# Filter in 64-row tiles and a folded first sequence: a Hyena convolution followed by routed experts on one Trainium2 core

## The chip, the cores and the metric

The kernel runs on one core of a Trainium2 chip. The core has a matrix engine (TensorE, PE in the rows; its weight loads are PEld), a vector engine (VectorE, DVE), a scalar engine (ScalarE, ACT), a general engine (GpSimd, POOL) and a queue engine that issues most DMAs (SyncE, SP). Each engine works through its own instructions in order; semaphores tie them together. The metric is the device time of one execution in microseconds.

## The reference

Two layers follow each other. The first is a long convolution over four sequences of 11456 tokens with 128 channels; the second sends every token to one of eight experts.

```python
h_mlp = np.maximum(pos_emb @ w1, 0.0) @ w2          # [S, 64] -> [S, 128]
h_filt = h_mlp * np.exp(-0.01 * pos)[:, None]
u = x * v
y = irfft(rfft(u, 2 * S) * rfft(h_filt, 2 * S))[:, :S, :]
x = (x * y).reshape(B * S, D)
logits = x @ w_gate + modality_bias[modality_id]
e_idx = argmax(logits); gate_w = softmax(logits)[e_idx]
out[e_idx == e] = gate_w * (np.maximum(x[e_idx == e] @ w1[e], 0.0) @ w2[e])
```

All inputs are float32, and the float32 matmuls of the convolution run on TensorE as two passes each: a weight load and a stream of moving columns, twice.

## The kernel before

**Transform.** The convolution is done by a two-step transform of length 90 x 64. A sequence lies as 2 blocks (`blk`) of 90 x 64 tokens, of which 45 pairs of places are held: partition `n` (0 to 63, 45 in use) has place `n`, and partition `64 + n` the mirrored place. The first step is a product with `fwd` (two halves, `c`, of 90 columns): the even part of the cosine table is the same for a place and its mirror, the odd part has the opposite sign (`shape_constants`). So one contraction over 128 partitions forms, in effect, sum and difference of the two halves and transforms them. The second step (`middle_stages`) works on groups of four of the 90 frequencies.

**Stages and their order.** The program is a list of steps, `seq`; a step calls small functions that issue instructions, and the order of these calls is each engine's order. The stages of the start are:

1. The filter's outer part (`filter_stages`, lines 515 to 551), 16 values of `q`. `load(q)` fetches 256 KB of embeddings on SP. `hidden(q)` multiplies with `wf[:, 1]`, in which w1 stands twice on the diagonal, 128 rows (line 528: four matmuls of 128 weight columns and 128 moving columns), and one DVE instruction applies ReLU and the window and leaves PSUM (line 532). `transform(q)` multiplies by `fwd` (line 542: four matmuls of 180 moving columns), and ACT copies the result to `A` (line 547). By `FOUT` a step issues load(t), hidden(t - 2) and transform(t - 3), in that order.
2. The filter's middle (`filter_middle`, lines 574 to 615), 23 groups: turn (line 581), spectrum (591, with the table B that `load_b` fetched into `A`, line 571), second (606, 64-row tiles, with w2 from `wf[:, 0]`); ACT and DVE copy (583, 594, 609 to 611), and POOL's queue writes each group's spectrum to DRAM (`hs`, line 612).
3. The forward transform of sequence 0 (`forward_stages(0)`, lines 480 to 514), 16 values of `q`. `load(q)` issues four DMAs on SP (lines 486 and 487, two each for u and v). `product(q)` is one DVE instruction, u times v (line 492). `transform(q)` does two halves, each 16 matmuls of 128 rows, 64 weight columns and 90 moving columns into a pair of PSUM banks (line 507), and ACT copies the half to `A` (line 510). There are two pairs of banks. Loads and products lie `F2` = 24 steps earlier, beside the filter's middle; there are 12 tiles for u and six halves of three output tiles (`xo`) for v.

`load_b(k)` stands in step k of `seq`, from 0 to 22. The memsets of `wg`, of three `xo` tiles and of twelve tiles (lines 441 to 445) are POOL's first work.

Then follow the middle stage of sequence 0 (`middle_stages(0)`), and for each further sequence its forward transform, middle stage, inverse transform and routing, interleaved. Routing writes rows to DRAM, and POOL scatters them to the experts' regions (`send_rows`).

**Experts.** `experts` works through tiles of 512 rows, eight chunks each (`hidden`, `result`). `rows_in(i + 2)` fetches rows on SP; `result` writes a tile's output to DRAM by four DMAs (line 1271) and reads it back turned (`y`, line 1273); ACT scales it two tiles later (line 1290), and POOL scatters it. Where a tile's rows lie stands in tables that DVE makes by some twenty short instructions each (`tile_table`). They are generators: at each chunk the loop takes one step of one of them (`next`), and `rows_in` runs them out when a tile needs its table. The last one, `rest()`, writes eight pads behind the experts' rows (lines 1052 to 1062) and then makes the last two tables.

Of the kernel before, what the change touches and what calls it, by code (L numbers as in the profile page):

```python
# [15 lines left out]
I32 = mybir.dt.int32  # L16
# [45 lines left out]
FMID = "turn:0 spectrum:1 second:3"  # L62
FIRST = "forward load product"
EA = 3
# [9 lines left out]
def apart(a, axis):  # L74

    out = np.zeros_like(a)
    n = np.arange(HALF)
    to, of = [slice(None)] * a.ndim, [slice(None)] * a.ndim
    to[axis], of[axis] = 4 * (n // 3) + n % 3, n
    out[tuple(to)] = a[tuple(of)]  # L80
    return out


# [16 lines left out]
def shape_constants():  # L100
# [28 lines left out]

    win = apart(win.reshape(2, 64, 2, N2), 1).transpose(2, 1, 3, 0)  # L130

# [59 lines left out]
def hyena_moe_kernel(ctx: ExitStack, tc: tile.TileContext, a: dict, out: bass.AP,  # L191
# [189 lines left out]
    with ExitStack() as cv:  # L381
# [25 lines left out]
        wf = keepp.tile([D, 2, D], F32, name="wf")  # L407
        dve.memset(wf, 0.0)
        wg = late_wg
# [15 lines left out]
        def constants():  # L425
            sp.dma_start(inv, a["c_inv"].rearrange("p (c n) -> p c n", c=2))
            sp.dma_start(small, a["c_small"])
            t = counts["tri"] = new_a("tri")[:, 0:2 * D]
            sp.dma_start(t, a["c_tri"])
            sp.dma_start(wg[:, 0:E], a["moe_w_gate"])  # L430
            sp.dma_start(bias, a["moe_modality_bias"].rearrange("m e -> (m e)")
                         .partition_broadcast(D).rearrange("p (m e) -> p m e", m=2))

        def split_constants():
            dve.tensor_copy(base, sm("reg"))
            dve.tensor_copy(score[:, E], sm("bad"))
            dve.memset(powers[:, E], 1e-9)
            dve.tensor_copy(both, counts.pop("tri"))
            free("tri")
# [35 lines left out]
        def forward_stages(b):  # L475
# [37 lines left out]

            return load, product, transform

        def filter_stages():
# [7 lines left out]
            def hidden(q):  # L524
                t = kept.pop((q, "emb"))
                m1 = bank("m1")
                for i in range(4):
                    pe.matmul(m1[:, D * i:D * i + D], t[:, D * i:D * i + D], wf[:, 1],
                              start=True, stop=True)
                free(("emb", q))  # L530
                r = new_a(("r", q))[:, 0:512].rearrange("p (m f) -> p m f", m=8)
                dve.scalar_tensor_tensor(
                    r, m1.rearrange("p (m f) -> p m f", m=8), 0.0,
                    win[:, q].unsqueeze(2).broadcast_to([D, 8, D // 2]),
                    op0=ALU.max, op1=ALU.mult)
                kept[q, 1] = r.rearrange("p (n b) f -> p n (b f)", b=2)

            def transform(q):
                r = kept.pop((q, 1))
                p = pair("s1")  # L540
                for j in range(4):
                    pe.matmul(p[:, j // 2, 2 * N1 * (j % 2):2 * N1 * (j % 2 + 1)],
                              r[:, j], fwd.rearrange("p c k -> p (c k)"), start=True, stop=True)
                free(("r", q))
                for h in range(2):
                    n0 = 4 * q + 2 * h
                    act.copy(A[:, :, 0].rearrange("p k (c n) -> p k c n", c=2)[:, :, :, n0:n0 + 2],
                             p[:, h, 0:4 * N1].rearrange("p (n c k) -> p k c n", n=2, c=2))

# [350 lines left out]
        def outer_steps(b):  # L900
# [13 lines left out]
            if b < nb:  # L914
                load, product, transform = forward_stages(b)
                todo |= {"load": load, "product": product, "forward": transform}
            if b == nb:
                todo.pop("places")
# [11 lines left out]
            if b == 0:  # L930
                ahead = lambda q: 2 * q if q < NA else q + F2 - NA
                when = {"load": ahead, "product": lambda q: ahead(q) + 2, "forward": lambda q: q + F2 - 1}
                return steps(NQ, [(when[n], todo[n]) for n in FIRST.split()])
            table = [w.split(":") for w in (LAST if b == nb else OUTER).split()]
# [113 lines left out]
    def rest():  # L1048


        assert not waiting and len(scatters) == nb * NR // D, (len(waiting), len(scatters))
        sp.dma_start(pad, a["c_pad"].rearrange("p (j r) -> p j r", j=TH // D))
        sp.dma_start(xs[E * R:E * R + TH, :].rearrange("(p j) r -> p j r", j=TH // D), pad)
        end = new("step", [1, E], I32)
        dve.tensor_copy(end, base[0:1])
        yield
        for e in range(E):
            v = nc.values_load(
                end[0:1, e:e + 1], engines=[ENG.SP], min_val=0, max_val=E * R - TH,
                skip_runtime_bounds_check_because="a region holds every token and a tile more")  # L1060
            after_all(sp.dma_start(xs[ds(v, TH), :].rearrange("(p j) r -> p j r", j=TH // D), pad),
                      scatters)
            yield
        dve.tensor_sub(nall, base[0:1], reg)
# [11 lines left out]
        tabs[nb] = new("tabh", [1, 3, NH], I32)  # L1076
        yield from tile_table(new, tabs[nb], took, start, left, NH, TH)

    outs, fetched = [], []
# [13 lines left out]
    def experts(lo, hi):  # L1093
# [212 lines left out]
        for at in range(len(work) + 6):  # L1306
# [45 lines left out]
def device_inputs(inputs):  # L1352
    arrays = {name: np.ascontiguousarray(inputs[name]) for name in _INS}
    tile4 = lambda a: a.reshape(D, 2, NQ, 4, -1).transpose(2, 0, 1, 3, 4).reshape(NQ, D, -1)
    held = np.r_[0:D:2, 1:D:4]
    chan8 = lambda a: (apart(a.reshape(2, 64, 2, N2, NQ, 8), 1).transpose(4, 2, 1, 0, 5, 3)
                       .reshape(NQ, D, -1)[:, held])
    for name, of, order in (("x", "x", tile4), ("u", "x", chan8), ("v", "v", chan8)):
        arrays[name] = np.ascontiguousarray(
            np.stack([order(spread(np.asarray(a))) for a in inputs[of]]))  # L1360

    pos = apart(spread(np.asarray(inputs["pos_emb"])).reshape(2, 64, 2, NQ, 4, -1), 1)
    arrays["pos_emb"] = np.ascontiguousarray(
        pos.transpose(3, 0, 5, 4, 2, 1).reshape(NQ, D, -1))
    ids = np.asarray(inputs["moe_modality_id"]).astype(np.int64, copy=False).reshape(B, S)
# [22 lines left out]
```

## Time and profile before

| what | value |
|---|---|
| median of 3 runs | 2089.98 us (2086.85 to 2091.12) |
| the profiled execution | 2090.39 us |
| its span, first to last instruction | 2088.5 us |
| PE, PEld, DVE, ACT, POOL busy | 97%, 79%, 80%, 60%, 62% |
| granted TensorE clock, mean | 0.994 |

The profile is that of one execution. An engine is busy while one of its compute instructions runs; matmuls are pipelined, so one's duration is longer than its distance to the next, and a stretch counts as busy when any runs. In the groups a line gives the source line, the engine, the operation, output and input, the shape and the count; behind the bar the busy time and the mean of one in ns, then the idle time before them and what ended it.

### The profile page before, as it was taken

The page shows a single profiled execution, that of the slowest core. Times are in us where ns is not written, and L with a number is a line of the kernel's source. Part 1 is how long each engine was busy: PE and PEld are TensorE (multiplying, and loading weights), DVE is VectorE, ACT ScalarE, POOL GpSimd, SP SyncE. Part 2 cuts the span into 40 slices and gives each one's busy share as a digit, 9 for nine tenths or more (in the row PEclk, how much of TensorE's full clock was granted, in tenths as well). Part 3 has the DMA queues.
Part 4 walks back from the last instruction along what each step waited for, and adds up shares of the span by engine and source line. Part 5 has one row for each costly group of instructions (what it writes and reads, how often), then busy time and mean ns, then how long its engine had stood idle before and what let it go on. Part 6 is the DMA issues. An engine that isn't in the chain of part 4 may idle for free. (4 is left out here: it accounts for less than half of the span.)

```text
span 2088.5 us, 50278 instructions
## 1 busy us (share of the span) xinstructions
PE 2020.7 (97%) x17794; PEld 1651.2 (79%) x17794; DVE 1670.4 (80%) x2690; ACT 1262.1 (60%) x2454; POOL 1286.7 (62%) x1426
## 2 busy tenths in 40 slices
PE   8999999999999999999999999999999899999997
PEld 8887877777778777777578888888888778888897
DVE  2528777896779867896987898888888798888885
ACT  3642376225752376325666777777777677777775
POOL 2219700697868777786758777777776344444554
PEclk9999999999999999999999999999999999999999
DMA  9846766668877788765896567666665555555310
GB/s 292 308 163 230 246 207 193 224 235 278 277 233 248 251 263 279 246 238 166 242 307 204 118 134 149 136 142 143 136 147 109 106 101 93 98 97 102 81 42 28
DMA packets 502937, 380.78 MB, mean 182 GB/s; under 512 B 374745, under 2 KB 408365, under 8 KB 502681
## 3 DMA queue, kind: packets, MB, share of 16 engines
q1 hardware_dynamic: 470265, 294.16, 52.1%
q0 software_dynamic: 32256, 83.33, 12.0%
q8 instruction: 142, 2.33, 0.5%
q14 instruction: 114, 0.93, 0.1%
q10 hardware_dynamic: 160, 0.03, 0.0%
HBM read 273.80 MB, written 103.96 MB: 181 GB/s over the span
## 5 line engine op out<-in xcount | busy, mean ns | idle before, releaser
L1242 DVE SCALAR_TENSOR_TENSOR hl<-ph,hh 128x512 fp32r<-128x512 f32 x724 | 489.7, 684 | 120.3 <-ACT hh L1241 109.1
L1294 POOL DMA_INDIRECT out<-ot,idx x362 | 389.6, 1076 | 295.7 <-issue 230.1
L1241 ACT ACTIVATE hh<-ph 128x512 fp32r<-128x512 f32 x724 | 422.9, 595 | 165.9 <-PE ph L1238 161.3
L284 POOL DMA_INDIRECT xs<-back,to x360 | 386.1, 1073 | 147.3 <-issue 88.9
L1259 PE MATMUL po<-hh,wh 128*128 128x512 f32 (+1 forms) x792 | 295.0, 372 | 7.4 <-ACT hh L1241 7.4
L1236 PE MATMUL ph<-xh,wh 128*128 128x512 f32 (+1 forms) x792 | 298.8, 377 | 1.1 <-ACT xh L1222 1.1
L1238 PE MATMUL ph<-xl,wh 128*128 128x512 f32 (+1 forms) x792 | 296.5, 374 | 3.4 <-DVE xl L1223 3.2
L1237 PE MATMUL ph<-xh,wl 128*128 128x512 f32 (+1 forms) x792 | 294.4, 372 | 1.0 <-DVE wl L1191 1.0
L1261 PE MATMUL po<-hl,wh 128*128 128x512 f32 (+1 forms) x792 | 294.7, 372 | 0.4 <-DVE hl L1242 0.3
L1260 PE MATMUL po<-hh,wl 128*128 128x512 f32 (+1 forms) x792 | 294.2, 371 | 0.0
L709 ACT COPY A<-pw 128x512 f32<-128x512 f32 x180 | 95.6, 584 | 289.1 <-PE pw L703 289.1
L703 PEld LDWEIGHTS pw<-rings,a 64*128 64x128 f32 x3952 | 227.1, 188 | 25.4 <-issue 7.9
L703 PE MATMUL pw<-rings,a 64*128 64x128 f32 x3952 | 238.6, 276 | 5.8 <-DMA rings<-in_c_c 1.7
L672 DVE TENSOR_TENSOR a<-pz,rings 128x1024 f32<-128x1024 f32 (+1 forms) x184 | 211.2, 1188 | 1.5 <-POOL a L679 1.5
L648 PE MATMUL pz<-A,rings 128*64 128x256 f32 x1440 | 169.9, 384 | 18.3 <-issue 12.4
L1259 PEld LDWEIGHTS po<-hh,wh 128*128 128x128 f32 x792 | 149.4, 189 | 33.8 <-ACT hh L1241 7.8
L1238 PEld LDWEIGHTS ph<-xl,wh 128*128 128x128 f32 x792 | 149.5, 189 | 32.6 <-DVE xl L1223 5.0
L507 PE MATMUL s<-fwd,a 128*64 128x90 f32 x4096 | 170.1, 242 | 1.4 <-issue 1.0
L1261 PEld LDWEIGHTS po<-hl,wh 128*128 128x128 f32 x792 | 149.4, 189 | 27.7 <-DVE hl L1242 1.7
L1237 PEld LDWEIGHTS ph<-xh,wl 128*128 128x128 f32 x792 | 149.7, 189 | 26.4 <-DVE wl L1191 1.3
L1236 PEld LDWEIGHTS ph<-xh,wh 128*128 128x128 f32 x792 | 149.5, 189 | 26.1 <-ACT xh L1222 1.3
L1260 PEld LDWEIGHTS po<-hh,wl 128*128 128x128 f32 x792 | 149.4, 189 | 25.4
(194 smaller groups left out, 3529.5 us busy)
## 6 DMA issues: line engine op xcount, KB each, us to landing
rings<-hs SPq DMA_DIRECT2D x88, 512.0 KB
a<-in_x SPq DMA_DIRECT2D x64, 512.0 KB
xr<-xo SPq DMA_DIRECT2D x64, 365.6 KB
back<-xr POOLq DMA_DIRECT2D x72, 325.0 KB
rings<-in_c_b SPq DMA_DIRECT2D x88, 256.0 KB
rings<-in_c_c SPq DMA_DIRECT2D x88, 256.0 KB
x<-xs SPq DMA_DIRECT2D x292, 64.0 KB
ob<-oT SPq DMA_DIRECT2D x292, 64.0 KB
```

Source lines behind the costliest of these rows:

```text
L284: s = pool.indirect_dma_start(out=xs, out_offset=bass.IndirectOffsetOnAxis(ap=ix, axis=0), in_=src, in_offset=None, bounds_check=E * R - 1 ...
L672: dve.tensor_mul(part[i], z[:, :, i].unsqueeze(1).broadcast_to([D, 2, n, 2, D]), h[:, 0].unsqueeze(3).broadcast_to([D, 2, n, 2, D]))
L703: pe.matmul(pw[par][:, to:to + D], t[at], k["c"][at, q, c], start=i == 0, stop=i == len(terms) - 1)
L1236: pe.matmul(p, k[0, "h"][:, f:f + D], k["xh"], start=True, stop=False)
L1237: pe.matmul(p, k[0, "l"][:, f:f + D], k["xh"], start=False, stop=False)
L1238: pe.matmul(p, k[0, "h"][:, f:f + D], k["xl"], start=False, stop=True)
L1241: act.activation(hh, ph, AF.Relu)
L1242: dve.scalar_tensor_tensor(hl, ph, 0.0, hh.bitcast(F32), op0=ALU.max, op1=ALU.subtract)
L1259: pe.matmul(po, k[1, "h"][:, f], hh[:, t], start=g == 0, stop=False)
L1260: pe.matmul(po, k[1, "l"][:, f], hh[:, t], start=False, stop=False)
L1261: pe.matmul(po, k[1, "h"][:, f], hl[:, t], start=False, stop=g == NCH - 1)
L1294: s = pool.indirect_dma_start(out=out, out_offset=bass.IndirectOffsetOnAxis(ap=k["idx"][:, j:j + 1], axis=0), in_=ot[:, j, :], in_offset=N ...
```

## The change

The filter's `hidden` uses 64-row tiles: w1 stands once in each half of the partitions, and each half's matmuls have 128 weight columns and 64 moving columns, into a bank of their own (two banks per q). Two DVE instructions of 256 columns take the place of one of 512; then POOL subtracts the halves and DVE adds them (256 columns each), and `transform` works on sum and difference, in 64-row tiles, with 90 moving columns. The input arrays are laid out for it on the way in: in the second half of the partitions the places that are mirrored.

For sequence 0 (`FOLDED = 1`) u times v is folded in the same way: POOL makes the difference, a new function `total` makes the sum on DVE, and the matmuls of `transform` are of 64 rows and 64 weight columns. Loads of q = 12 to 15 come at steps 2q, products eight steps later for q < 12, totals one step after them.

The loads of w1 and w2 are one DMA each (w1 on SP, ahead of the embeddings). `load_b` moves to steps 10 to 21, two a step. The memsets come one at a time in steps 2 to 17. In `rest()` the two tables come ahead of the pads, and it starts 11 tiles ahead of its due tile where it was 7.

```diff
-FIRST = "forward load product"
+FIRST = "forward load product total"
+FOLDED = 1
+def mirrored(a):
+    return np.concatenate([a[:, :, :, :, :, :1], a[:, :, ::-1, :, :, 1:]], 5)
         def first_constants():
-            for j in range(2):
-                half = slice(64 * j, 64 * j + 64)
-                act.dma_start(wf[half, 1, half], a["w1"])
-            for j in range(2):
-                pool.dma_start(wf[64 * j:64 * j + 64, 0], a["w2"])
+            sp.dma_start(wf[:, 1, 0:64], a["w1"])
             pool.dma_start(win, a["c_win"].rearrange("p (q m) -> p q m", q=NQ))
             pool.dma_start(fwd, a["c_fwd"].rearrange("p (c k) -> p c k", c=2))
+            pool.dma_start(wf[:, 0], a["w2"])
-        pool.memset(wg, 0.0)
-        for t in xo_t:
-            pool.memset(t.rearrange("p w s h r -> p (w s h r)")[:, 0:2048], 0.0)
-        for t in tiles:
-            pool.memset(t[:, 512:1024], 0.0)
+        blank = [wg, *(t.rearrange("p w s h r -> p (w s h r)")[:, 0:2048] for t in xo_t),
+                 *(t[:, 512:1024] for t in tiles)]
             def product(q):
...
+                if b < FOLDED:
+                    pool.tensor_sub(u[:, 512:1024], u[:, 0:512], u[:, 512:1024])
+            def total(q):
+                u = kept[q, "u"]
+                if b < FOLDED:
+                    dve.scalar_tensor_tensor(u[:, 0:512], u[:, 0:512], 2.0, u[:, 512:1024],
+                                             op0=ALU.mult, op1=ALU.subtract)
             def transform(q):
...
-                                pe.matmul(v[64 * c:64 * c + 64, blk, j], u[:, blk, 4 * h + j],
-                                          fwd[:, c], start=True, stop=True)
+                                if b < FOLDED:
+                                    at = slice(64 * blk, 64 * blk + 64)
+                                    x, w = u[at, c, 4 * h + j], fwd[at, c]
+                                else:
+                                    x, w = u[:, blk, 4 * h + j], fwd[:, c]
+                                pe.matmul(v[64 * c:64 * c + 64, blk, j], x, w, start=True, stop=True)
             def hidden(q):
                 t = kept.pop((q, "emb"))
-                m1 = bank("m1")
+                m = [bank("m1") for _ in range(2)]
                 for i in range(4):
-                    pe.matmul(m1[:, D * i:D * i + D], t[:, D * i:D * i + D], wf[:, 1],
-                              start=True, stop=True)
+                    for b in range(2):
+                        at = slice(64 * b, 64 * b + 64)
+                        pe.matmul(m[b][:, 64 * i:64 * i + 64], t[at, D * i:D * i + D],
+                                  wf[at, 1, 0:64], start=True, stop=True)
...
+                of = rings[:, 1024 * (q % 5):1024 * (q % 5) + 1024]
+                r = of[:, 0:512].rearrange("p (i b f) -> p i b f", b=2, f=64)
+                for b in range(2):
+                    dve.scalar_tensor_tensor(
+                        r[:, :, b], m[b][:, 0:256].rearrange("p (i f) -> p i f", f=64), 0.0,
+                        win[:, q, 4 * b:4 * b + 4].unsqueeze(2).broadcast_to([D, 4, 64]),
+                        op0=ALU.max, op1=ALU.mult)
+                pool.tensor_sub(of[:, 768:1024], of[:, 0:256], of[:, 256:512])
+                dve.tensor_add(of[:, 512:768], of[:, 0:256], of[:, 256:512])
+                kept[q] = of[:, 512:1024].rearrange("p (c n x) -> p c n x", c=2, n=2)
             def transform(q):
...
+                for j in range(2):
+                    for c in range(2):
+                        for x in range(2):
+                            at, to = slice(64 * x, 64 * x + 64), N1 * (2 * j + c)
+                            pe.matmul(p[:, x, to:to + N1], r[at, c, j], fwd[at, c],
+                                      start=True, stop=True)
...
             if b == 0:
-                ahead = lambda q: 2 * q if q < NA else q + F2 - NA
-                when = {"load": ahead, "product": lambda q: ahead(q) + 2, "forward": lambda q: q + F2 - 1}
+                ahead = lambda q: 2 * q
+                when = {"load": ahead, "product": lambda q: 2 * q + (10 if q < NA else 4),
+                        "total": lambda q: 2 * q + (11 if q < NA else 5),
+                        "forward": lambda q: q + F2 - 1}
         for k in range(NG):
-            seq[k] = lambda f=seq[k], k=k: (f(), load_b(k))
+            at = 10 + k // 2
+            seq[at] = lambda f=seq[at], k=k: (f(), load_b(k))
+        for k, t in enumerate(blank):
+            seq[k + 2] = lambda f=seq[k + 2], t=t: (f(), pool.memset(t, 0.0))
     def rest():
+        ...  # the two tables, as they stood behind the pads
         sp.dma_start(pad, a["c_pad"].rearrange("p (j r) -> p j r", j=TH // D))
...
-        ...  # the two tables
-            for k, first, end in ((1, 2, NW[0]), (2, NW[0], NW[1]), (3, NW[2] - 7, NW[2])):
+            for k, first, end in ((1, 2, NW[0]), (2, NW[0], NW[1]), (3, NW[2] - 11, NW[2])):
```

## Rows read from the trace of the kernel before

**Rows 1.** The page: busy time of each engine, share of the span, instructions.

```profile
PE 2020.7 (97%) x17794; PEld 1651.2 (79%) x17794; DVE 1670.4 (80%) x2690; ACT 1262.1 (60%) x2454; POOL 1286.7 (62%) x1426
```

**Rows 2.** Busy time by stage; columns: stretch, length, engines, PEclk, DMA share, GB/s.

```profile
6.40:42.40 36.00, 35.88 (x256) 35.63 (x256) 11.42 (x20) 12.55 (x31) 8.62 (x14) 1.00 1.04 311
42.40:102.50 60.10, 58.09 (x630) 52.54 (x631) 28.25 (x55) 38.62 (x70) 11.13 (x21) 1.00 0.85 306
102.50:145.10 42.60, 40.49 (x1026) 40.00 (x1026) 7.90 (x8) 24.68 (x33) 1.16 (x3) 1.00 0.51 170
```

**Rows 3.** Groups by line and form, first 90 us.

```profile
L528 PE MATMUL m<-wf,a 128*128 128x128 f32 x128 | 18.5, 294 | 6.5 <-DMA wf<-in_w 6.5
L606 PEld LDWEIGHTS ph<-wf,rings 64*128 64x128 f32 x266 | 16.2, 187 | 2.0
...
L492 DVE SCALAR_TENSOR_TENSOR a<-a,small,xo 128x1024 f32<-128x1024 f32 x8 | 10.2, 1274 | 0.0
...
L611 DVE TENSOR_TENSOR rings<-ph,rings 128x256 f32<-128x256 f32 x16 | 6.6, 413 | 0.0
L445 POOL MEMSET a<- 128x512 f32 x12 | 5.7, 582 | 0.0
L443 POOL MEMSET xo<- 128x2048 f32 x3 | 5.4, 1860 | 0.0
```

**Rows 4.** Groups by line and form, 102.5 to 145.1 us.

```profile
L507 PEld LDWEIGHTS s<-fwd,a 128*64 128x64 f32 x1024 | 40.0, 137 | 1.9 <-issue 1.9
L510 ACT COPY A<-s 128x720 f32<-128x720 f32 x32 | 24.3, 760 | 17.2 <-PE s L507 17.2
```

**Rows 5.** Order of time, 0 to 30 us; columns: start, length, engine, line, count.

```profile
6.48 3.75 PE L528 MATMUL m<-wf,a 128*128 128x128 f32 x16 [6.48 <-DMA wf<-in_w]
...
15.46 1.01 PEld L528 LDWEIGHTS m<-wf,a 128*128 128x128 f32 x8
...
17.57 1.01 PEld L528 LDWEIGHTS m<-wf,a 128*128 128x128 f32 x8
```

**Rows 6.** Order of time, 40 to 66 us: one second() of the filter's middle.

```profile
48.41 0.97 PEld L606 LDWEIGHTS ph<-wf,rings 64*128 64x128 f32 x16
```

**Rows 7.** Order of time on ACT, 1600 to 1716 us: the scaling of y.

```profile
1627.04 1.28 ACT L1290 ACTIVATE ot<-y,ends 128x128 f32<-128x128 f32 x4
1637.92 1.28 ACT L1290 ACTIVATE ot<-y,ends 128x128 f32<-128x128 f32 x4
...
1669.68 1.28 ACT L1290 ACTIVATE ot<-y,ends 128x128 f32<-128x128 f32 x4 [9.67 <-DMA y<-ob]
...
1702.30 1.28 ACT L1290 ACTIVATE ot<-y,ends 128x128 f32<-128x128 f32 x4
1714.42 1.27 ACT L1290 ACTIVATE ot<-y,ends 128x128 f32<-128x128 f32 x4
```

**Rows 8.** Order of time on SP's queue, 1637 to 1675 us.

```profile
1643.77 2.14 SPq L1271 DMA_DIRECT2D ob<-oT  x4
...
1648.48 2.69 SPq L1061 DMA_DIRECT2D xs<-pad  x2
...
1654.69 2.24 SPq L1061 DMA_DIRECT2D xs<-pad  x2
...
1662.96 0.38 SPq L1061 DMA_DIRECT2D xs<-pad  x1
...
1667.06 0.34 SPq L1273 DMA_DIRECT2D y<-ob  x1
```

**Rows 9.** Line 794 (logits, 32-column tiles): durations min/median/max in ns.

```profile
L794 PEld LDWEIGHTS pl<-rings,wg x248: 106/108/109, 274.0 to 1039.4; 128*32 128x32 f32 x124
```

**Rows 10.** Order of time on DVE, then on POOL, 186 to 196 us.

```profile
189.66 4.39 DVE L678 TENSOR_TENSOR a<-a,a 128x512 f32<-128x512 f32 x1
...
190.87 0.73 POOL L667 TENSOR_TENSOR a<-a 128x256 f32<-128x256 f32 x1
...
192.23 1.27 POOL L679 TENSOR_TENSOR a<-a,a 128x512 f32<-128x512 f32 x1
```

**Rows 11.** Order of time on PE, 274 to 276 us: one logits().

```profile
274.05 0.94 PE L794 MATMUL pl<-rings,wg 128*32 128x436 f32 x8
```

More of the change, by code (lines that the diff above doesn't have):

```diff
@@ L128, in shape_constants @@
     win = np.where(there, np.exp(np.float32(-0.01) * pos.astype(np.float32)), 0)
-    win = apart(win.reshape(2, 64, 2, N2), 1).transpose(2, 1, 3, 0)
+    win = mirrored(apart(win.reshape(2, 64, 2, NQ, 2, 2, 1), 1)).transpose(5, 1, 3, 0, 2, 4, 6)
     order = lambda a: a.reshape(D, 2, NO, 8).transpose(0, 2, 1, 3).reshape(D, NO * NC)
@@ L407, in hyena_moe_kernel @@
         wf = keepp.tile([D, 2, D], F32, name="wf")
-        dve.memset(wf, 0.0)
         wg = late_wg
@@ L427, in constants @@
             sp.dma_start(small, a["c_small"])
-            t = counts["tri"] = new_a("tri")[:, 0:2 * D]
+            t = counts["tri"] = rings[:, 5 * 1024:5 * 1024 + 2 * D]
             sp.dma_start(t, a["c_tri"])
@@ L438, in split_constants @@
             dve.tensor_copy(both, counts.pop("tri"))
-            free("tri")
-        pool.memset(wg, 0.0)
-        for t in xo_t:
-            pool.memset(t.rearrange("p w s h r -> p (w s h r)")[:, 0:2048], 0.0)
-        for t in tiles:
-            pool.memset(t[:, 512:1024], 0.0)
+        blank = [wg, *(t.rearrange("p w s h r -> p (w s h r)")[:, 0:2048] for t in xo_t),
+                 *(t[:, 512:1024] for t in tiles)]
         ring_of = {name: [rings[:, at:at + size] for at in places] for name, size, places in (
@@ L512, in transform @@
                 free(("u", q))
-            return load, product, transform
+            return load, product, total, transform
         def filter_stages():
@@ L530, in hidden @@
                 free(("emb", q))
[L531 to L536, printed above, removed]
+                of = rings[:, 1024 * (q % 5):1024 * (q % 5) + 1024]
+                r = of[:, 0:512].rearrange("p (i b f) -> p i b f", b=2, f=64)
@@ L538, in transform @@
             def transform(q):
-                r = kept.pop((q, 1))
+                r = kept.pop(q)
                 p = pair("s1")
[L541 to L548, printed above, removed]
+                for j in range(2):
[4 more added lines that the diff above has]
+                                      start=True, stop=True)
@@ L550, in filter_stages @@
+                for x in range(2):
+                    act.copy(A[:, :, 0].rearrange("p k (c n) -> p k c n", c=2)[:, :, :, 4 * q + x:4 * q + 4:2],
+                             p[:, x, 0:4 * N1].rearrange("p (n c k) -> p k c n", n=2, c=2))
             todo = dict(hidden=hidden, transform=transform, load=load)
@@ L914, in outer_steps @@
             if b < nb:
-                load, product, transform = forward_stages(b)
+                load, product, total, transform = forward_stages(b)
                 todo |= {"load": load, "product": product, "forward": transform}
+                if b < FOLDED:
+                    todo["total"] = total
             if b == nb:
@@ L930, in outer_steps @@
             if b == 0:
-                ahead = lambda q: 2 * q if q < NA else q + F2 - NA
-                when = {"load": ahead, "product": lambda q: ahead(q) + 2, "forward": lambda q: q + F2 - 1}
-                return steps(NQ, [(when[n], todo[n]) for n in FIRST.split()])
+                ahead = lambda q: 2 * q
+                when = {"load": ahead, "product": lambda q: 2 * q + (10 if q < NA else 4),
+                        "total": lambda q: 2 * q + (11 if q < NA else 5),
+                        "forward": lambda q: q + F2 - 1}
+                return steps(NQ, [(when[n], todo[n]) for n in FIRST.split() if n in todo])
             table = [w.split(":") for w in (LAST if b == nb else OUTER).split()]
@@ L1048, in rest @@
     def rest():
[L1051 to L1063, printed above, removed]
         dve.tensor_sub(nall, base[0:1], reg)
@@ L1077, in rest @@
         yield from tile_table(new, tabs[nb], took, start, left, NH, TH)
+        assert not waiting and len(scatters) == nb * NR // D, (len(waiting), len(scatters))
+        sp.dma_start(pad, a["c_pad"].rearrange("p (j r) -> p j r", j=TH // D))
+        sp.dma_start(xs[E * R:E * R + TH, :].rearrange("(p j) r -> p j r", j=TH // D), pad)
+        end = new("step", [1, E], I32)
+        dve.tensor_copy(end, base[0:1])
+        yield
+        for e in range(E):
+            v = nc.values_load(
+                end[0:1, e:e + 1], engines=[ENG.SP], min_val=0, max_val=E * R - TH,
+                skip_runtime_bounds_check_because="a region holds every token and a tile more")
+            after_all(sp.dma_start(xs[ds(v, TH), :].rearrange("(p j) r -> p j r", j=TH // D), pad),
+                      scatters)
+            yield
     outs, fetched = [], []
@@ L1353, in device_inputs, with chan8 @@
     arrays = {name: np.ascontiguousarray(inputs[name]) for name in _INS}
-    tile4 = lambda a: a.reshape(D, 2, NQ, 4, -1).transpose(2, 0, 1, 3, 4).reshape(NQ, D, -1)
+    tile4 = lambda a, b: a.reshape(D, 2, NQ, 4, -1).transpose(2, 0, 1, 3, 4).reshape(NQ, D, -1)
     held = np.r_[0:D:2, 1:D:4]
-    chan8 = lambda a: (apart(a.reshape(2, 64, 2, N2, NQ, 8), 1).transpose(4, 2, 1, 0, 5, 3)
-                       .reshape(NQ, D, -1)[:, held])
+    def chan8(a, b):
+        a = apart(a.reshape(2, 64, 2, N2, NQ, 8), 1)
+        if b < FOLDED:
+            a = np.stack([a[0], a[1][:, ::-1]]).transpose(4, 0, 1, 2, 5, 3)
+        else:
+            a = a.transpose(4, 2, 1, 0, 5, 3)
+        return a.reshape(NQ, D, -1)[:, held]
     for name, of, order in (("x", "x", tile4), ("u", "x", chan8), ("v", "v", chan8)):
         arrays[name] = np.ascontiguousarray(
-            np.stack([order(spread(np.asarray(a))) for a in inputs[of]]))
-    pos = apart(spread(np.asarray(inputs["pos_emb"])).reshape(2, 64, 2, NQ, 4, -1), 1)
+            np.stack([order(spread(np.asarray(a)), b) for b, a in enumerate(inputs[of])]))
+    pos = mirrored(apart(spread(np.asarray(inputs["pos_emb"])).reshape(2, 64, 2, NQ, 2, 2, -1), 1))
     arrays["pos_emb"] = np.ascontiguousarray(
-        pos.transpose(3, 0, 5, 4, 2, 1).reshape(NQ, D, -1))
+        pos.transpose(3, 0, 6, 2, 4, 5, 1).reshape(NQ, D, -1))
+    for name in ("w1", "w2"):
+        arrays[name] = np.concatenate([arrays[name]] * 2)
     ids = np.asarray(inputs["moe_modality_id"]).astype(np.int64, copy=False).reshape(B, S)
```

## The prediction

> **What bounds the kernel now.** TensorE is busy 97% of the span [rows 1], but that share is no bound for this change: the edits sit in the first 145 us and at one place near 1640 us. I first cut the span into its stages [rows 2]: the filter's first layer and transform (6.4 to 42.4), the filter's middle (42.4 to 102.5), the first sequence's forward transform (102.5 to 145.1). TensorE fills all three, while DVE works 11.4, 28.3 and 7.9 us and POOL 8.6, 11.1 and 1.2; so each stage is as long as its matmuls. The groups by line [rows 3, 4] give the prices of one instruction, the order of time [rows 5, 6] the distance between passes. Each fp32 matmul is two passes. In 128-row tiles one q of the filter (eight passes of 128 and eight of 180 columns) takes 17.57 - 15.46 = 2.11 us [rows 5]. Last I read the waits near the pads: ACT's L1290 comes every 10.88 us until 1637.92, then 76.50 us later for the sixth time where 65.28 were due: 11.2 us are lost there, most of it in one wait of 9.67 us for y [rows 7], which SyncE issues late because eight pad writes stand ahead of it [rows 8].
>
> The changes are therefore worth what the new bound of each stage is, not what the array saves. The sum goes against the profiled execution, 2090.39 us (span 2088.5 and 1.9 around it), 0.4 above the median of the three runs.
>
> **Start.** The first matmul begins at 6.48 and waits for w1 [rows 5], two DMAs on ACT's queue (lines 415 to 417). Now w1 is one DMA at the head of SP's queue, the first embedding behind it, and no table load of B ahead. I take 5.0, so -1.5; from 0 (w1 lands no earlier) to -2.5. The first 16 passes take 3.75 us [rows 5], twice the later time; I leave that cost as it is.
>
> **Filter, per q.** A hidden layer is now 16 passes (64 rows, 128 weight columns, 64 moving columns), the transform 16 passes of 64 rows, 128 weight columns, 90 moving columns. Two row tiles run side by side: sixteen L606 weight loads span 0.97 us, (0.97 - 0.19)/15 = 0.052 apart [rows 6], 0.104 to 0.11 per tile, of the same 128 weight columns. Is that the load or the 128 moving columns? Loads last 0.108, 0.137 and 0.187 us for 32, 64 and 128 columns [rows 3, 4, 9]: 0.8 ns a column, about 0.107 for 128. So fewer moving columns don't help: 8 passes x 0.111 = 0.89 for either, 1.78 for both. If the load were hidden, 64 and 90 columns at L507's rate (0.039 a pass for two tiles of 90) would give 0.45 + 0.62 = 1.1; if it costs more than read, 2.1.
>
> But the transform of q now waits for a longer chain: 0.2 until the last pass is out (a pass lasts 0.29, the next comes after 0.11), two DVE ops of 256 columns 0.78, then DVE's add 0.41 and POOL's subtract 0.73 [rows 3, 10], and 0.1 for signals. Do add and subtract run together? In the stretch after 189 us a DVE subtract with two SBUF operands (0.69 by size) took 4.39 us and ended 0.55 after POOL's run of SBUF operations [rows 10]: they exclude each other. So the chain is 0.2 + 0.78 + 0.41 + 0.73 + 0.1 = 2.2 us. Between hidden(q) and transform(q) TensorE has transform(q-1) and hidden(q+1) only; over two periods it does one q's work and waits out one chain: (1.78 + 2.2)/2 = 1.99. That is 0.12 less than 2.11, -1.9 over 16. The sixteen memsets, moved in between POOL's subtracts, fit (0.73 + 0.58 < 1.99) but for three of 1.86 us [rows 3, 10]: +1.2. The last transform has nothing under its chain: +0.8. With the start: -1.5 - 1.9 + 1.2 + 0.8 = **-1.4 us**. From -7 (period 1.65) to +5.
>
> My sum leaves the memsets out of the exclusion, because they read nothing; if they take part, each add also waits out a memset, the period is 2.27 for twelve q and 2.95 for three, and that is the +5.
>
> The Trainium skill tells of that exclusion too (SBUF — State Buffer, "SBUF: two separate sides") and limits it, for a DVE instruction with two SBUF inputs, to GpSimd work that reads SBUF. By that rule the +5 can't come about. No run here shows a memset beside such an add.
>
> **Loads.** The 23 loads of B (one DMA each) stand in steps 10 to 21 instead of 0 to 22. Embeddings and B are 39 x 262 KB = 10.2 MB, at the stage's 311 GB/s [rows 2] 33 us: landed by 37, the first wanted at 42. Costs nothing; without that cover, 0.8 us each. The u, v loads (four DMAs each) of q = 0 to 5 follow, and then SP waits for product(0), eight steps later than before. From there one q (2 x 384 KB = 0.79 MB) and two spectra (1.05 MB) per 5.14 us are the demand of before.
>
> **Forward of sequence 0.** Passes go from 128 rows x 64 columns to 64 x 64. Now 1024 take 40.0 us, 0.039 each, with two tiles in flight [rows 4]. With four, 16 q's halves take 32/4 x 0.078 = 0.62 us of TensorE, and L510 (0.76) follows in two buffers: (0.62 + 0.17 + 0.76 + 0.1)/2 = 0.82 a half, 26 us in all. Four column tiles run together: eight logits passes of 436 columns (363 ns each at 90 columns per 75 ns) take 0.94 us, two passes' time [rows 11]. Row and column tiles together stand in no row.
>
> The Trainium skill (TensorE: Matmul & The Clock Gate, "Part 3: Packing small matmuls — row/col tiling") says that they compose. By that rule (c) below falls away. No run here shows it, and (c) has its chance from the column tiles alone.
>
> So 42.6 - 27 = -15 if operands were there. They aren't. Per q DVE has product (1.27), POOL the subtract (1.27 for 512 columns, row of L679), DVE the total, 0.70 (an estimate between L611's 0.41 for 256 and L492's 1.27 for 1024) [rows 3, 10]. Until step 42 this hides in the filter's middle (two groups, 5.14 us, for 3.3). At the first forward step, F, seven products are done; nine must follow. Order on DVE: t6, p7, t7, p8, t8, then p9 p12 t9 t12, p10 p13 t10 t13, p11 p14 t11 t14, p15, t15. Alone, one q is 1.27 + 0.1 + 1.27 + 0.1 + 0.70 = 3.4; a pair, POOL and DVE excluding each other, 2 x (1.27 + 1.27 + 0.70) = 6.4. From F + 1.6 (DVE's last spectrum): t6 2.3, t8 9.2, t9/t12 15.6, t10/t13 22, t11/t14 28.4, t15 31.7. Forward(10) waits to F + 21.3, (11) to F + 27.7; then five of 1.63 and the last copy: F + 36.6, 37 with a slower clock behind the idle. Against 42.5: **-5.5 us**. Without the exclusion t11 comes at F + 21: -9. With DVE never late: -15. With one tile pair in flight, -0.5. u, v of 12 to 15 wait for forward(0) to (3), land by F + 8 to 18, before their products.
>
> **Pads.** Table first, then pads: rest() yields 51 times before the first pad, so at one step per chunk the eight pads go from tile 53 to tile 55, chunk 3, on. In SP's order there are now five pads, the rows of a tile, and three pads between one y and the next ob, where 1643.77 to 1667.06 has five, the rows and one. At 1.9 us a pad [rows 8] y comes 23 us after the ob before it, as now; but the first ob is no longer late, and the second table, which is now drained in one go at 1697 (1714.42 - 1702.30 is 1.24 too long [rows 7]), is ready. -0.8 - 1.2 = **-2 us**; from +4 to -11.
>
> Sum: 2090.39 - 1.4 - 5.5 - 2.0 = **2081.5 us**. Everything behind 145 us moves up with it: the middle stage that follows starts on rings whose loads follow those of u and v, landed by F + 25.
>
> **Rivals.** (a) As summed, 2081.5, from 2077 to 2087: 0.52. (b) TensorE sets the pace: loads hidden in the filter or no exclusion in the forward stage, 4 + 3.5 less: 2074. For it: DVE idles in both stages now; against: the 4.39 us [rows 10]. 0.14. (c) The 64 x 64 tiles don't run four at a time: forward 42 instead of 37, 2086.5. For it: no row shows it; against: the logits. 0.13. (d) The pads no longer hold y up: 9 more, 2072. For it: the 9.67 is one collision; against: the count of pads between. 0.09. (e) Slower: the folding's chain p, subtract, t becomes longer than the stage it shortens. Each product not done by F costs 3.4 us; seven should be done. If loads of q = 6 on, released only at step 30, land so late that three or fewer are, t11 comes 13.6 us later and the time is 2095; it turns slower than before from about three products late. For it: the loads' eight-step shift; against: transfers run at 306 GB/s in that stage, and its demand from product(0) on is unchanged. 0.10. (f) The edits change nothing that counts: 2090. 0.02.
>
> A measurement of this kernel tells some 0.2%, 4.2 us, from no change. Faster by more: most of (a) 0.45, (b) 0.14, (d) 0.09, a third of (c): 0.72. Slower: (e) and a rest, 0.12. Same: 0.16. The range takes (b) and (d) at its low end and (f) at the high: 2072 to 2091.
>
> **What would show it.** Right: hidden and transform at 0.9 us per q and a gap before the transform, period 2.0; forward halves 0.82 apart to q = 9, then two gaps of 4 to 5 us before forward(10) and (11) that DVE ends; a wait for y near 10 us two tiles later. Wrong: a period below 1.8 (loads hidden, no exclusion), halves at 1.24 (tiles not in fours), products behind a DMA, no wait for y.

## The result, and the profile after

The changed kernel takes 2109.9 us (median of 4 runs) where the kernel before takes 2090.3 beside it: ratio 1.0095, 95% interval 1.0077 to 1.0112. It is slower, and far outside the range of 2072 to 2091. The profiled execution took 2106.84 us, span 2104.9, 16.4 above the span before. Of the experiments, four were timed on a chip where the kernel before took 2247 to 2288 us (they are marked); of these the first 150 us of the trace are read and the totals are not used. One kernel was timed there and on another chip: its forward stage takes 36.4 us on the one and 36.3 on the other. One kernel (called filled steps) took 2107 to 2111 us in three runs and 2142 in two, and its trace is of one of the two.

First the stages of the changed kernel, the answer to [rows 2]: stretch, length, busy us of each engine, granted clock, DMA share, GB/s.

```profile
4.00:60.80 56.80, 55.33 (x512) 54.89 (x512) 19.80 (x52) 12.42 (x30) 24.79 (x32) 1.00 0.90 272
61.70:124.70 63.00, 60.26 (x630) 54.57 (x630) 27.89 (x57) 38.79 (x68) 19.06 (x27) 1.00 0.64 232
124.70:162.20 37.50, 29.05 (x1024) 25.87 (x1024) 22.14 (x22) 24.02 (x33) 16.59 (x12) 0.87 0.59 200
```

The filter's first layer and transform, 36.0 us before, take 56.8, and TensorE is busy in 55.3 of them. It waits once, for 1.4 us; for the rest the passes themselves are slow. The order of time on TensorE (start, length, line, count), as in [rows 5]:

```profile
4.04 3.68 PE L541 MATMUL m<-wf,a 64*128 64x64 f32 x32 [4.04 <-DMA a<-in_pos_emb]
7.48 1.99 PE L562 MATMUL s<-fwd,rings 64*128 64x90 f32 x16
9.24 1.89 PE L541 MATMUL m<-wf,a 64*128 64x64 f32 x16
10.90 1.98 PE L562 MATMUL s<-fwd,rings 64*128 64x90 f32 x16
12.65 1.89 PE L541 MATMUL m<-wf,a 64*128 64x64 f32 x16
14.32 0.69 PE L562 MATMUL s<-fwd,rings 64*128 64x90 f32 x4
16.43 1.59 PE L562 MATMUL s<-fwd,rings 64*128 64x90 f32 x12 [1.42 <-POOL rings L551]
```

One q takes 12.65 - 9.24 = 3.41 us, where 2.11 was the time before: 1.7 for the hidden layer, 1.7 for the transform, each eight pairs of passes, so 0.213 a pair. In [rows 5] only the first 16 passes ran at such a rate (3.75 us); here all 512 do. The groups by line and form (busy us, mean ns of one), first 125 us, put the same 64-row, 128-weight-column tile at two rates:

```profile
L562 PE MATMUL s<-fwd,rings 64*128 64x90 f32 x256 | 31.6, 424 | 1.4 <-POOL rings L551 1.4
L541 PE MATMUL m<-wf,a 64*128 64x64 f32 x256 | 29.9, 413 | 4.0 <-DMA a<-in_pos_emb 4.0
L624 PE MATMUL ph<-wf,rings 64*128 64x128 f32 x360 | 26.3, 285 | 1.2 <-DVE rings L629 1.2
```

L624, in the filter's middle, streams more columns (128) in less time (285 ns, pairs 0.11 apart). The granted clock reads 1.00 in the filter all the same; *Started warm* below shows how far that column can be read. The ledger against before, from the first and last pass of each stage (the forward stage up to the first pass of the middle of sequence 0): start -2.4, filter +20.9 (56.7 for 35.9), middle +2.5 (61.5 for 59.0; its first two steps still run at the slow rate), wait ahead of the forward stage +1.4, forward stage -5.1 (37.4 for 42.5), all that follows -0.7. The sum is 16.6, or 16.4 with the gap ahead of the middle, 0.1 shorter, and rounding.

At the pads, ACT's scaling of y, the answer to [rows 7]:

```profile
1687.53 1.27 ACT L1315 ACTIVATE ot<-y,ends 128x128 f32<-128x128 f32 x4
1709.72 1.28 ACT L1315 ACTIVATE ot<-y,ends 128x128 f32<-128x128 f32 x4 [11.21 <-DMA y<-ob]
1720.10 1.28 ACT L1315 ACTIVATE ot<-y,ends 128x128 f32<-128x128 f32 x4
...
1741.86 1.27 ACT L1315 ACTIVATE ot<-y,ends 128x128 f32<-128x128 f32 x4
```

From 1687.53 to 1741.86 are 54.3 us where four times 10.88 were due: 10.8 lost, against 11.2 before. The drain is gone (the later ones come 10.4 and 10.9 us apart), and the wait for y has grown from 9.67 to 11.21. On SP's queue, the answer to [rows 8]:

```profile
1678.53 2.06 SPq L1296 DMA_DIRECT2D ob<-oT  x4
...
1699.13 3.97 SPq L1100 DMA_DIRECT2D xs<-pad  x3
...
1706.84 0.34 SPq L1298 DMA_DIRECT2D y<-ob  x1
```

This y is issued 28.3 us after the ob of the tile before it; in [rows 8] it was 23.3 (1643.77 to 1667.06).

### The profile page after: what moved, and what is told of

Its sections match the earlier page's. It is cut to its first block, busy times and chain, and to the rows that moved or that the text cites. A ratio compares the mean times of both kernels' runs of the same rounds, so it can differ in the third digit from the quotient of the medians.

```text
span 2104.9 us, 50899 instructions
## 1 busy us (share of the span) xinstructions
PE 2030.8 (96%) x18050; PEld 1658.5 (79%) x18050; DVE 1691.8 (80%) x2737; ACT 1262.5 (60%) x2454; POOL 1321.3 (63%) x1457
## 5 line engine op out<-in xcount | busy, mean ns | idle before, releaser
L666 PE MATMUL pz<-A,rings 128*64 128x256 f32 x1440 | 171.4, 388 | 16.5 <-issue 10.8
L519 PE MATMUL s<-fwd,a 128*64 128x90 f32 (+1 forms) x4096 | 158.7, 249 | 9.0 <-ACT A L521 3.9
```

## Experiments

**Theory.** In the filter TensorE stays at 1.2 GHz, the lower of its two levels, because of what its stream is made of. Rivals: 64-row tiles with fewer moving than weight columns are that slow at any clock; waits near 15 us kept the clock from rising; the loss comes from the loads and products put off.

**Filter as before.** All of the change but the filter's tiles and the loads of their weights.

```diff
-    pe.matmul(m[b][:, 64 * i:64 * i + 64], t[at, D * i:D * i + D], wf[at, 1, 0:64], ...)
+    pe.matmul(m1[:, D * i:D * i + D], t[:, D * i:D * i + D], wf[:, 1], ...)
...
-    pe.matmul(p[:, x, to:to + N1], r[at, c, j], fwd[at, c], ...)
+    pe.matmul(p[:, j // 2, ...], r[:, j], fwd.rearrange("p c k -> p (c k)"), ...)
```

> The changed kernel with the filter's hidden layer and transform in 128-row tiles again (block-diagonal w1, no sum and difference), everything else of the change kept. Theory, the filter's 64-row passes run at half rate: the filter's last transform ends near 43 to 46 us, not 60.8, the forward stage of sequence 0 keeps its 37 us, and the time is 2087 to 2092. Rival, the loss lies in the loads and products that were put off: the time stays above 2103.

2088.0 us, ratio 0.9995 (0.9986 to 1.0005); the last transform ends at 42.6 (42.4 before). All the loss is the filter's. It also shows what the rest is worth: next to nothing. The forward stage takes 39.5 us, 3.0 less than before, behind a wait of 1.8 (0.15 before).

**Filter alone.** The kernel before with the filter's tiles, their loads and the blanks of the change.

> The kernel before with the filter's part of the change alone (64-row tiles, sum and difference, the blanks put behind the steps). Theory, half rate: hidden layer and transform take about 1.7 us each per step, the last transform ends near 60 us, the time is 2105 to 2112. Rival, the loss lies in the loads and products: the filter takes what it took, the time is 2086 to 2093.

2111.65 us, ratio 1.0109 (1.0092 to 1.0125); the last transform ends at 62.5. As the theory has it.

**Hidden layer in 128-row tiles**, the transform as changed.

```diff
-    for b in range(2): pe.matmul(m[b][:, 64 * i:64 * i + 64], t[at, D * i:D * i + D], wf[at, 1, 0:64], ...)
+    pe.matmul(m[:, D * i:D * i + D], t[:, D * i:D * i + D], wf[:, 1], ...)   # block-diagonal w1
```

> The changed kernel with the hidden layer alone in 128-row tiles (128 moving columns), the transform still in 64-row tiles with 90 moving columns. Theory, the half rate is TensorE's lower clock, which the whole stream sets: both kinds of pass have one rate, either 0.11 us (period near 2.0, time 2087 to 2093) or, if the hidden layer does not lift it, 0.21 us (period 3.4, time near 2110). Rival, a 64-row tile with fewer moving than weight columns takes 0.21 us by itself: hidden 0.9, transform 1.7, period 2.6 us, time 2094 to 2099.

2094.4 us, ratio 1.0028 (1.0015 to 1.0042). Groups by line and form, then the order of time:

```profile
L542 PE MATMUL m<-wf,a 128*128 128x128 f32 x128 | 19.6, 302 | 5.7 <-DMA wf<-in_w 5.7
L564 PE MATMUL s<-fwd,rings 64*128 64x90 f32 x256 | 19.3, 283 | 4.0 <-POOL rings L553 3.4 <-DVE rings L554 0.4
```

```profile
31.81 1.16 PE L542 MATMUL m<-wf,a 128*128 128x128 f32 x8
32.90 1.13 PE L564 MATMUL s<-fwd,rings 64*128 64x90 f32 x16
33.96 1.16 PE L542 MATMUL m<-wf,a 128*128 128x128 f32 x8
```

This decides against the first rival: the transform's passes, unchanged, go from 424 to 283 ns because another line's passes changed. The rate belongs to the stream, not to the tile. The total missed its 2087 to 2093. The trace shows two losses: 3.4 us of waits for GpSimd, whose blanks stand ahead of its subtract, and 33.96 - 31.81 = 2.15 us a step, no less than the 2.11 in 128-row tiles alone: 1.09 + 1.06 where 0.89 each were due.

**Filled steps.** One 128-row matmul with 512 moving columns more per step, its result overwritten.

```diff
     m = [bank("m1") for _ in range(2)]
+    pe.matmul(m[0], t[:, 0:D], t, start=True, stop=True)
```

> The changed kernel with one matmul more in each of the 16 filter steps: 128 rows, 128 weight and 512 moving columns, its result overwritten. Theory, lower clock: with the array filled in between, the 64-row passes go at 0.11 us, a step takes 0.9 + 0.9 + 0.4 = 2.2 us, the time falls to 2088 to 2096 although there is more work. Rival, the 64-row passes are slow by themselves: a step takes 3.4 + 0.4 us, the time rises to 2115 to 2118.

2107.3 to 2110.8 us, ratio 1.0086 (1.0066 to 1.0106): neither. The trace has every pass slow, the added ones too (two of 512 columns in 2.0 us), and a step takes 5.7. So full-array work in the stream doesn't lift the clock each time; what the runs of 2107 us did isn't traced.

**Started warm** (on the marked chip). Six matmuls on zeros, result unused, ahead of the first hidden layer.

```diff
+    heat = rings[:, 11 * 512:12 * 512]
+    dve.memset(heat, 0.0)
+    hot = bank("m1")
+    for _ in range(6):
+        pe.matmul(hot, heat[:, 0:D], heat, start=True, stop=True)
```

> The changed kernel with six more matmuls (128 rows, 128 weight and 512 moving columns, zeros, result unused) on TensorE ahead of the first hidden layer. Theory, the filter's own stream can't keep TensorE at 2.4 GHz: its 64-row passes fall back to 0.21 us soon after the start and the time is that of the changed kernel plus the delay of the first pass, 2110 to 2116. Rival, the stream only never gets up because of its waits in the first 16 us: started at the full rate it stays at 0.11 us, a step takes 2 us, the time is 2090 to 2097.

Order of time on TensorE; stretches as in the stages above; groups by line and form, 22 to 60 us:

```profile
16.90 0.91 PE L567 MATMUL s<-fwd,rings 64*128 64x90 f32 x12 [0.41 <-POOL rings L556]
17.64 1.04 PE L546 MATMUL m<-wf,a 64*128 64x64 f32 x16
18.51 0.41 PE L567 MATMUL s<-fwd,rings 64*128 64x90 f32 x4
19.44 1.46 PE L567 MATMUL s<-fwd,rings 64*128 64x90 f32 x12 [0.52 <-POOL rings L556]
20.68 1.88 PE L546 MATMUL m<-wf,a 64*128 64x64 f32 x16
22.34 1.97 PE L567 MATMUL s<-fwd,rings 64*128 64x90 f32 x16
```

```profile
9.05:19.40 10.35, 8.53 (x133) 7.76 (x132) 5.33 (x14) 2.52 (x6) 8.37 (x11) 1.00 1.05 323
20.68:60.23 39.55, 39.54 (x371) 39.31 (x368) 13.86 (x37) 9.92 (x24) 12.78 (x18) 0.50 0.84 253
```

```profile
L567 PE MATMUL s<-fwd,rings 64*128 64x90 f32 x192 | 23.4, 423 | 0.0
L546 PE MATMUL m<-wf,a 64*128 64x64 f32 x166 | 19.6, 412 | 0.0
```

The hidden layer's 16 passes take 1.04 us until 18, 1.88 from 20.7 on, and stay so to the end of the filter (60.2), though no wait follows. Here the clock itself is seen: the granted clock falls from 1.00 to 0.50 at 19.6 and stays there to 67.4, in the filter's middle. Started at 2.4 GHz, the stream falls to 1.2 and doesn't come back. The second rival falls, and once more the first: until 18 the 64-column passes go at the upper rate.

This also tells what slowed the changed kernel. Its passes take 424 and 413 ns, and at a granted clock of 0.50 the same passes take 423 and 412 here. So its filter ran at 1.2 GHz, although the column reads 1.00 there. In the changed kernel's trace the column first falls at 124.3, and it reads 1.00 over all that lies before, the slow passes too; only from a trace's first fall on does it tell the level.

**Wider hidden layer** (marked chip). 128 moving columns, half of the result unused.

```diff
-    pe.matmul(m[b][:, 64 * i:64 * i + 64], t[at, D * i:D * i + D], wf[at, 1, 0:64], ...)
+    pe.matmul(m[b][:, D * i:D * i + D], t[at, D * i:D * i + D], wf[at, 1], ...)   # w1 twice
```

> The changed kernel with 128 instead of 64 moving columns in the hidden layer's 64-row tiles (w1 twice side by side; the second 64 result columns are not used); the middle of the filter has 64-row tiles of just this shape at 0.11 us a pass. Theory A, what the lower clock follows is how few columns are streamed per loaded weight: the wider pass lifts the clock, hidden layer and transform take 0.9 us each, a step 1.8 to 2.0 us, the time is 2083 to 2090. Theory B, it takes 128-row tiles in the stream, as the hidden layer alone in 128-row tiles had: the passes stay at 0.21 us and the time near 2110.

Order of time on TensorE, and one stretch:

```profile
15.46 1.40 PE L563 MATMUL s<-fwd,rings 64*128 64x90 f32 x12 [2.15 <-POOL rings L552]
16.65 1.99 PE L542 MATMUL m<-wf,a 64*128 64x128 f32 x16
18.42 1.50 PE L563 MATMUL s<-fwd,rings 64*128 64x90 f32 x16
19.75 1.09 PE L542 MATMUL m<-wf,a 64*128 64x128 f32 x16
```

```profile
15.80:19.00 3.20, 3.20 (x34) 3.02 (x30) 0.34 (x1) 0.83 (x2) 3.20 (x8) 0.50 1.12 341
```

Twice the moving columns in 0.6 of the time: 16 hidden passes take 1.09 us (1.89 in the changed kernel), a step 1.9. Here too the clock falls behind a gap, to 0.50 at 15.7 and the passes to 1.99, but at 19.1 it is back. So theory B falls: no 128-row tile is in this stream, and it goes at the upper level; the hidden layer's moving columns are all that differs on TensorE from the changed kernel. Theory A fits, but it is not shown as a rule: the filled steps streamed more columns per loaded weight than the changed kernel too, and their trace is slow. The filter still ended at 44.1, with 4.0 us of waits behind GpSimd's blanks.

**Repaired.** The wider hidden layer once more, with the blanks written by VectorE.

```diff
-    for k, t in enumerate(blank): ... pool.memset(t, 0.0)
+    dve.memset(wg, 0.0)   # and xo, ahead of the first hidden layer
+    for k, t in enumerate(blank): ... dve.memset(t, 0.0)
```

> The changed kernel with the hidden layer's 64-row tiles 128 moving columns wide and the blanks written by VectorE (four ahead of the first hidden layer, one per step after it) instead of GpSimd. Theory, with the clock up and GpSimd free the filter goes at 1.9 us a step without a wait: the last transform ends near 39 us (42.4 in the kernel before), the middle of sequence 0 begins 4 to 6 us earlier than in the kernel before, the time is 2083 to 2087. Rival, VectorE's writes take the place of GpSimd's wait, or the put-off products give it all back ahead of the forward stage: 2088 to 2091.

2086.25 us beside 2090.55, ratio 0.9975 (0.9966 to 0.9984): it beats both kernels. Groups by line and form:

```profile
L544 PE MATMUL m<-wf,a 64*128 64x128 f32 x256 | 19.0, 294 | 4.7 <-DMA a<-in_pos_emb 4.7
L565 PE MATMUL s<-fwd,rings 64*128 64x90 f32 x256 | 18.7, 276 | 0.9 <-DVE rings L555 0.6
```

The transform's passes, 424 ns in the changed kernel, take 276. Order of time:

```profile
10.73 1.03 PE L565 MATMUL s<-fwd,rings 64*128 64x90 f32 x16
11.59 1.09 PE L544 MATMUL m<-wf,a 64*128 64x128 f32 x16
12.52 1.17 PE L565 MATMUL s<-fwd,rings 64*128 64x90 f32 x16
...
34.69 1.09 PE L544 MATMUL m<-wf,a 64*128 64x128 f32 x16
```

Twelve steps lie between 11.59 and 34.69: one is (34.69 - 11.59)/12 = 1.93 us, the last transform ends at 38.6 (42.4 before), and the middle of sequence 0 begins at 140.5 (145.1 before).

**Early products**, first with the filter as before (marked chip), then again for its time, then on the repaired kernel.

```diff
-    ahead = lambda q: 2 * q
-    when = {"load": ahead, "product": lambda q: 2 * q + (10 if q < NA else 4), "total": ... + 1, ...}
+    ahead = lambda q: 2 * q if q < NA else q + F2 - NA
+    when = {"load": ahead, "product": lambda q: ahead(q) + 2, "total": lambda q: ahead(q) + 3, ...}
```

> The filter in 128-row tiles as before, the loads and products of sequence 0 and the loads of the first matrices at the steps they had before (12 products ahead of the forward stage, each total one step behind its product), the folded forward stage and the pads' edit as changed. Theory, the put-off products hold the folded forward stage (39.5 us with the filter as before): with 12 of 16 done earlier it goes at ScalarE's pace of 0.82 us per half, 27 to 31 us, and the time is 2076 to 2081. Rival, the added subtractions and totals then hold up the filter's middle, or the gain is waited for again in the middle of sequence 0: 2085 to 2090.

> The kernel with the filter in 128-row tiles and the products of sequence 0 early once more, for its time beside the other two: its trace had the middle of sequence 0 begin 4.3 us earlier than in the kernel before, so 2084 to 2087; rival, the 4.3 us are waited for again later, 2088 to 2091.

> The same with the loads and products of sequence 0 at the steps of the kernel before (each total one step behind its product). Theory, the transfers now bound all that lies ahead of the middle of sequence 0 (their share was 0.9 and more from 10 to 126 us with the products early), so the forward stage ends 1 to 3 us earlier than in the kernel with GpSimd freed alone: 2081 to 2086. Rival, TensorE's own 28 us bound the forward stage: it ends 6 us or more earlier, 2076 to 2080.

The loads of B go back to one a step with them. The first had its forward stage in 36.4 us, not 27 to 31. Timed again: 2086.7, ratio 0.9983 (0.9971 to 0.9996), forward stage 36.3. On the repaired kernel 2087.3, ratio 0.9981 (0.9969 to 0.9992), outside the 2081 to 2086 expected and no better than repaired alone, although its middle of sequence 0 begins at 139.3, 1.2 us earlier; where that is lost again is open. Early products and the repair don't add up. Order of time on TensorE in the forward stage of the second:

```profile
119.72 1.32 PE L518 MATMUL s<-fwd,a 64*64 64x90 f32 x57 [0.95 <-issue]
121.30 1.51 PE L518 MATMUL s<-fwd,a 64*64 64x90 f32 x64 [0.26 <-ACT A L520]
123.03 0.38 PE L518 MATMUL s<-fwd,a 64*64 64x90 f32 x6 [0.22 <-ACT A L520]
125.18 4.25 PE L518 MATMUL s<-fwd,a 64*64 64x90 f32 x122 [1.77 <-issue]
```

Two halves take 1.73 us (121.30 to 123.03), but there is a gap that no releaser explains ("issue") each 127 passes (57 + 64 + 6), at no border of the work. Columns as in the stages above:

```profile
112.00:130.00 18.00, 13.38 (x476) 11.49 (x469) 8.58 (x8) 11.07 (x16) 6.07 (x4) 0.91 0.81 277
130.00:140.50 10.50, 7.86 (x320) 6.89 (x318) 0.00 (x0) 7.37 (x11) 0.00 (x0) 1.00 0.02 5
```

The gaps of 0.95 and 1.77 us lie where DMA is busy 0.81; at 0.02 the one that is left is 0.28. From 103 to 140.5 us the instruction queue (packets, MB) has

```profile
q8 instruction: 8, 0.13, 1.3%
```

8 packets of 16 KB for 1024 weight loads and 1024 passes, one per 256 instructions, the distance of the gaps. That TensorE waits there for its program behind the data is read from this, and no run tested it.

**Pads alone** on the kernel before (first on the marked chip, then again).

> The kernel before with the pads' edit alone (tables first, then pads, four steps earlier). By the prediction: -2.0 us, 2087 to 2088, the drain ahead of the last tables gone and the wait for y 1.2 us shorter. Rival, read from the changed kernel's trace: the wait for y comes back in another place, -0.6 us, 2089 to 2090.

> The kernel before with the pads' edit alone, once more, since the first run of it fell on a chip whose times scatter by 1%. By the prediction: -2.0 us, 2088 where the kernel before takes 2090, the wait for y near 1664 gone or two tiles later and 1.2 us shorter. Rival, read from the changed kernel's trace: TensorE still stands still once for about 9 us at the pads, nothing or -0.6 us, 2089 to 2091.

Timed again: 2089.5 beside 2090.35, ratio 0.9996 (0.9986 to 1.0005): no change that can be told. ACT waits 10.86 us for y at 1689.36.

## Why the prediction was wrong

**The step that failed** is the price of a pass in the filter: "So fewer moving columns don't help: 8 passes x 0.111 = 0.89 for either, 1.78 for both." It measured 1.7 for either. 0.111 was taken from L606, whose tiles load the same columns, in a stream at 2.4 GHz. I treated the rate as the tile's, and asked only whether the load or the stream is longer; the runs show that the clock sets it, and that the stream decides on the clock. At the upper level the price itself was right: 0.87 for a hidden layer in the warm start (17.64 to 18.51), 0.93 and 0.86 in the repaired kernel (11.59 to 12.52, 10.73 to 11.59). [Rows 5] held the sign, the first 16 passes at twice the later time, and I wrote "I leave that cost as it is" instead of asking what ended it. PEclk gave no warning: it reads 1.00 in the filter before and after. None of my rivals had the clock in it. What in a stream brings the clock up stays open: with a hidden layer of 128 moving columns it came up, in 64-row and in 128-row tiles, with one of 64 it didn't.

**The chain** of 1.99 us a step was never reached in the changed kernel, where TensorE needs 3.4. In the repaired kernel, with the clock up, the step is 1.93, within 0.06; 1.79 of it are the passes (1.78 was taken). For the memsets between the subtracts the sum had +1.2. GpSimd ran three of them in one go (5.29 us from 9.46), which cost 1.4 us in the changed kernel, behind slow passes, and 4.0 with the wider hidden layer. Beside them VectorE's add took 0.42 us at 11.93, as ever: the +5 bound falls. The Trainium skill (SBUF — State Buffer, "SBUF: two separate sides") limits the exclusion of such an add to GpSimd work that reads SBUF, and the trace agrees.

**Start:** it gave -2.4 where -1.5 was taken, inside its bounds.

**Forward stage:** four 64 x 64 tiles do run together (rival c falls), halves are 0.87 apart where 0.82 was taken, and the pairs of products and totals came in the order forecast, with the mutual exclusion read from [rows 10]. VectorE in the changed kernel, then GpSimd:

```profile
146.23 2.47 DVE L490 SCALAR_TENSOR_TENSOR a<-a,small,xo 128x1024 f32<-128x1024 f32 x2
149.85 2.35 DVE L502 SCALAR_TENSOR_TENSOR a<-a 128x512 f32<-128x512 f32 x2 [1.15 <-POOL a L496]
```

```profile
147.58 3.47 POOL L496 TENSOR_TENSOR a<-a 128x512 f32<-128x512 f32 x2 [2.42 <-DVE a L490]
```

A pair of subtracts of 1.27 each takes 3.47, a pair of totals of 0.70 each 2.35. The stage gave -5.1 where -5.5 was forecast, and that is luck: the changed kernel had a longer filter and middle to prepare in, and its time is made of other terms. Ahead of forward(10) and (11) TensorE waited 0.35 and 1.50 us where 4 to 5 each were forecast. Two "issue" gaps took 0.53 and 2.57. And the clock fell twice:

```profile
124.77:131.10 6.33, 6.17 (x157) 5.93 (x160) 3.96 (x6) 3.41 (x5) 3.60 (x4) 0.50 0.86 324
151.75:154.95 3.20, 3.20 (x88) 3.20 (x92) 1.76 (x3) 1.28 (x2) 1.27 (x1) 0.50 0.03 8
```

At 1.73 us per 64 these 245 passes would take 6.6 us instead of 9.5, so the lower clock cost some 3 us (an estimate from these rows), where the sum had 0.4. With the filter as before the stage gave -3.0, and a wait for the last spectra took back 1.7. With the products early 36.3 us remained, with the granted clock at 0.50 for some 7 of them, so lateness was the smaller part.

**Loads** "costs nothing": DMA stood at 0 GB/s from 60 to 70 us, and nothing waited for B. Rival (e) is not what happened: the filter as before, with the loads as changed, is not slower.

**Pads:** -2.0 was forecast, none came. The term that failed is "y comes 23 us after the ob before it, as now": the three pads behind the rows, where one stood, were counted, but the time was left at that of six pads; y came 28.3 us after it (28.6 with the pads alone, 1658.12 to 1686.69). So the longer wait took back what the drain and the first ob gave.

## What to carry to other kernels

Packing small tiles saves array time only while the array's clock stays up: price a pass from a stream like the new one, not from a tile like it elsewhere. Where the profile shows the same pass at two rates, find what ended the slow stretch before counting on the fast one. Don't trust a granted clock of 1.00 ahead of the first fall in a trace. A stage that stays fully busy and still gets longer is read from the distance between passes, not from waits.

## What was not expected of the hardware

- TensorE was busy 55.3 of 56.8 us, and its passes stayed at the rate that they have at 1.2 GHz. The Trainium skill (TensorE: Matmul & The Clock Gate, "Part 1: The HAM clock gate (the "warmup" mystery)") lets sustained matmul activity release the clock; here TensorE worked without a wait from 16.4 us to the end of the filter at 60.8, and it was not released: the measurement decides.
- In the warm start the clock fell behind a gap of 0.52 us (gaps of 0.4 before it had none; whether the gap or the stream made it, no run separates), and it didn't come back in 40 us without a wait. It rose at 67.4, after 6 us of the middle's 128-row passes. The wider stream fell behind a gap of 2.15 us, at 15.7, and was back at 19.1.
- A change between 128-row and 64-row passes costs about 0.2 us each, an estimate: in the kernel with the hidden layer in 128-row tiles, hidden layer and transform take 1.09 and 1.06 us, where 0.89 and 0.86 are taken in streams of one kind (before; repaired).
- "Issue" gaps each 127 passes of up to 3.3 us (filter as before, at 130.42) while DMA is busy; the slower passes of before had one, of 1.0 us.
